# The first two gate/up pairs of the first 1024 tokens as four units of seven block products, run in phases

## The chip, the cores and the metric

One core of one Trainium2 chip runs the whole program. The metric is the device time of one execution in microseconds (us). A core has five engines with a queue each: PE multiplies matrices, DVE and ACT work on rows, POOL and SP mostly start transfers (DMAs). Each queue runs in its own order; semaphores make one wait for another.

## The reference

For 2048 tokens of width 1024 the reference mixes a local attention and a gated MLP, token by token:

```python
g = sigmoid((x * gate_w).sum(-1, keepdims=True))
qkv = x @ wqkv                                   # 32 heads of 32, window of 8 keys, every second token
a = attention(q, k, v) @ wo
b = (gelu(x @ w_gate) * (x @ w_up)) @ w_down     # inner width 3584
out = g * a + (1 - g) * b
```

All is in bf16, and `gelu` is the tanh form.

## The kernel before

**Tiles and stages.** The tokens are taken in two halves of 1024 (`SUP`), each half as two chunks of 512 columns (`SC`). The inner width of 3584 is cut into 14 pairs of 256 columns. First come the gate and up products of pair 0 and pair 1 for the first 1024 tokens, then queries and keys, values, and the rest of the pairs; then `down` (L1070) multiplies with `w_down` and `wo`. Large tiles lie in one tile called arena, at places given in KB (the R_ constants). PSUM, where PE writes, is one tile of eight banks, each 128 x 512 in f32.

**Seven block products.** A `Unit` (L360) multiplies a 256-column stripe of weights with 1024 tokens as a 2 x 2 block product with seven products instead of eight: L11, L12, L22 are blocks of the weights, S1 to S4 sums of blocks (`sums_pair`, L318), and R11, R12, R21, R22 are blocks of the transposed tokens, with T1 to T4 their differences (`x_forms`, L196, and `x_form3`). A product is four matmuls of 128x128 by 128x512. Its methods come in the order `p1` (L11), `p5` (S1), `p26` (L12 and S2), `p73` (S3 and S4) and `p4` (L22). Between them ACT copies a bank into another bank, where the next product is added to it (L384, L396), or into SBUF (L389, L374). In `p73` DVE adds one SBUF tile to two banks at once (L403): its operand is one access pattern that steps from bank Z to bank Y. `p4` adds into bank Y again, so it comes after this.

**The head.** `load_xn` brings rows of tokens, `pe_transpose_chunk` (L208) transposes 128x128 pieces on PE, four to a group, into one of four banks in turn, and DVE and ACT take turns to copy a group into SBUF (L219, L217). Pair 0 is computed plainly by `plain_pair` (L240), eight products for each 512 tokens: chunk 0 is transposed, multiplied, chunk 1 is transposed, and multiplied (L342 to L348). In between are `patterns` (small constant tiles), `x_forms`, `sums_pair` for pair 1, `gate_chunk` (the token gate's product) and `h_store` (gelu times up, L253). SP issues the loads in the order of the code: tokens of chunk 0, pair 0 in halves of 128 columns (256-byte rows), tokens of chunk 1, pair 1 in whole (512-byte rows), four blocks of the query/key weights (L336), and sixteen transposing loads of the other 1024 tokens (L340). Of these SP may have eight under way, since eight semaphores go round.

**The loop over units** (L1249) then runs all units with an overlap of one: `p1` of a unit, `p73` of the one before, `p5`, `p26`, `p4` of the one before. Pair 1 is its units 0 and 1 (`Q0` = 2), the queries and keys begin with unit 2. After each unit `run_bg` (L442) lets background tasks for DVE take steps, in order of priority, until a credit of 4.7 to 4.8 us is spent, by costs that the tasks state. `due` forces a task to its end ahead of a unit. Among the tasks are `sums_qk` (L456, sums of query/key weight blocks, priority 1), `h_task`, `late_forms`, `qk_prods` (products of queries and keys, L598) and `t_forms` (L864, differences of `w_down` blocks, L874), which has the lowest priority. `tf_close` (L886), at the end of unit `Q0` + 11, runs what is left of its first five steps at once.

Of the kernel before, what the change touches and what calls it, by code (L numbers as in the profile page):

```python
# [68 lines left out]
def kernel(  # L69
# [33 lines left out]
    def reg(kb, n):  # L103
        o = int(kb * KB)
        return arena[:, o:o + n]
# [12 lines left out]
    def bank(i):  # L118
        return banks[:, i, :]
# [17 lines left out]
    with tc.manual_schedule(engines={mybir.EngineType.PE, mybir.EngineType.DVE, mybir.EngineType.Activation,  # L137
# [11 lines left out]
        for i in range(NWARM):  # L149
            pw = bank(2 + i % 3)  # L150
            nc.tensor.matmul(pw, lhsT=warm[:, 0:P], rhs=warm, start=True, stop=True)
# [9 lines left out]
        sums1 = reg(R_W0 + 16, 4 * 2 * HK * P).rearrange("p (f m k n) -> p f m k n", f=4, m=2, k=HK)  # L161

        def load_pair(dst, i, split=False):
            c0 = 2 * P * i
            for (a, b) in (((0, P), (P, 2 * P)) if split else ((0, 2 * P),)):
                for m, src in ((0, B_w_gate), (1, B_w_up)):
                    nc.sync.dma_start(out=dst[:, m, :, a:b],
                                      in_=src[:, c0 + a:c0 + b].rearrange("(k p) n -> p k n", p=P))
# [3 lines left out]
        load_pair(raw0, 0, True)  # L172
        load_xn(1)
        load_pair(raw1, 1)
# [31 lines left out]
        ne = [0]  # L206

        def pe_transpose_chunk(c, dst):  # L208
            for j in range(4):
                for k0 in range(0, KT, 4):  # L210
                    p_ = bank((6, 7, 1, 5)[ne[0] % 4]).bitcast(BF16)[:, 0:SC].rearrange("p (a b) -> p a b", a=4)
                    for kk in range(4):
                        nc.tensor.transpose(out=p_[:, kk, :], in_=xn[c % 2][:, j, (k0 + kk) * P:(k0 + kk + 1) * P],
                                            identity=ident[:])
                    d = dst[:, k0:k0 + 4, j * P:(j + 1) * P]
                    if ne[0] % 2 == 1:
                        nc.scalar.copy(out=d, in_=p_)  # L217
                    else:
                        V.tensor_copy(out=d, in_=p_)  # L219
                    ne[0] += 1  # L220
# [12 lines left out]
        p5_n = [0]  # L233
# [5 lines left out]

        def plain_pair(w, G, U, s, half, xc):  # L240
            cs = slice(half * SC, (half + 1) * SC)
            for f in range(2):
                pg, pu = bank((0, 5)[f]), bank((3, 4)[f])
                for kt in range(KT):
                    nc.tensor.matmul(pg, lhsT=w[:, 0, kt, f * P:(f + 1) * P], rhs=xc[:, kt, :],
                                     start=(kt == 0), stop=(kt == KT - 1))
                nc.scalar.activation(out=G[:, f, cs], in_=pg, func=ACT.Gelu_apprx_tanh)
                for kt in range(KT):
                    nc.tensor.matmul(pu, lhsT=w[:, 1, kt, f * P:(f + 1) * P], rhs=xc[:, kt, :],
                                     start=(kt == 0), stop=(kt == KT - 1))  # L250
                nc.scalar.copy(out=U[:, f, cs], in_=pu)  # L251
# [16 lines left out]
        def patterns():  # L268
            with nc.allow_low_precision("block pattern of zeros and ones"):
                V.tensor_reduce(out=R_[:], in_=ident[:].rearrange("p (h d) -> p h d", d=4), axis=AX.X, op=ALU.add)  # L270
            pgw = bank(7).bitcast(BF16)[:, 0:KT]
# [63 lines left out]
        for i, (col, k0) in enumerate(((0, 0), (0, HK), (D, 0), (D, HK))):  # L335
            nc.sync.dma_start(out=wq[i], in_=A_wqkv[k0 * P:(k0 + HK) * P, col:col + D].rearrange("(k p) n -> p k n", p=P))  # L336
# [16 lines left out]

# [6 lines left out]
        class Unit:  # L360
# [15 lines left out]
            def p1(self):  # L376
                f = self.f
                self.T = self.dst()
                n = self.n
                self.X = bank((0, 5)[n % 2] if two[0] or n < Q0 else 0)  # L380
                self.yi = (2, 4)[n % 2]
                self.V, self.Y, self.Z = bank(1), bank(self.yi), bank(3)
                self.mm(self.X, "L11", f.R11, True)
                nc.scalar.copy(out=self.Y, in_=self.X)  # L384

            def p5(self):
                self.mm(self.V, "S1", self.f.T1, True)
                self.p5s = p5_tile()
                nc.scalar.copy(out=self.p5s, in_=self.V)  # L389

            def p26(self):
                f = self.f
                self.mm(self.X, "L12", f.R21, False)
                self.evac(self.T[:, 0, c1s], self.X)
                self.mm(self.Y, "S2", f.T2, False)
                nc.scalar.copy(out=self.Z, in_=self.Y)  # L396

            def p73(self):
                f = self.f
                self.mm(self.Y, "S3", f.T3, False)  # L400
                self.mm(self.Z, "S4", f.R22, False)
                pair = _win_ap(self.Z, [[(self.yi - 3) * SC, 2], [1, SC]])
                TT(out=self.T[:, :, c2s], in0=pair,  # L403
                   in1=self.p5s.rearrange("p (o n) -> p o n", o=1).to_broadcast([P, 2, SC]), op=ALU.add)
# [94 lines left out]
        def add_gu(w, sm, i, s):  # L499
            tg = tu = st_tile  # L500
            if i == 1 and s == 0:
                tg, tu = lambda: reg3(R_PROD, 2, SUP), lambda: reg3(R_PROD + 4, 2, SUP)
            ug = add_unit(gu_forms(w, sm, 0), xf[s], "gate", tg)
            uu = add_unit(gu_forms(w, sm, 1), xf[s], "up", tu)
            uu.fin = lambda: bg(h_task(ug.T, uu.T, i, s), *((5.5, now[0]) if (i, s) == (NPAIR - 1, 0) else (7.5 if i == NPAIR - 1 else 0, now[0] + 1)))
# [743 lines left out]
        for b in range(n):  # L1249
# [4 lines left out]
            prv = units[b - 1] if b > 0 else None  # L1254
            cur.p1()
            if prv:
                prv.p73()
# [11 lines left out]
            if prv:  # L1269
                prv.p4()  # L1270
# [37 lines left out]
```

## Time and profile before

| What | us |
|---|---|
| median of 3 runs (lowest, highest) | 720.98 (720.17, 722.09) |
| the profiled execution | 720.06 |
| its span, first to last instruction | 718.3 |
| PE busy in the span | 707.2 |
| DVE busy in the span | 673.2 |
| ACT busy in the span | 328.7 |
| first matmul of pair 0, of pair 1 (from the span's start) | 7.41, 25.06 |

A row of a timeline gives the start, the length, the engine, the line, what is done on which tiles, and how many instructions are merged; in brackets stands how long the engine sat idle before and what ended that. Matmuls are pipelined, so eight of 0.38 us each take less than eight times that; the distance from row to row is what they cost.

### The profile page before, as it was taken

Reading aid. Unit: us, or ns where it says so; the run is one execution under the profiler, and the core shown is the slowest. Engines: PE = TensorE matmul, PEld = TensorE weight load, DVE = VectorE, ACT = ScalarE, POOL = GpSimd, SP = SyncE. Lnnn points to the kernel's source line nnn. Section 1 sums busy time; section 2 is a strip of 40 time slices with the busy share of each in tenths; the row PEclk is TensorE's granted clock in tenths of the full one; section 3 lists DMA queues with packets and bytes.
Section 4 is the critical chain, followed back from the end, with each engine's and each line's share of the span. In section 5 each row is a group of like instructions: output and inputs, shape, how many; then the busy total and the mean of one; then the engine's idle time right before and its main releaser. Section 6 shows DMA issues by size and latency. Waiting matters only on the chain. (4 is left out here: it accounts for less than half of the span.)

```text
span 718.3 us, 10752 instructions
## 1 busy us (share of the span) xinstructions
PE 707.2 (98%) x4051; PEld 408.2 (57%) x4107; DVE 673.2 (94%) x722; ACT 328.7 (46%) x600; POOL 134.5 (19%) x233
## 2 busy tenths in 40 slices
PE   8999999999999999999999999999999999999998
PEld 4466656655544444444444444444447886758887
DVE  2789989999999999999999999999999999899997
ACT  4554546444456665555555555555322321131431
POOL 1323544133210332121300000000210002110011
PEclk9999999999999999999999999999999999999999
DMA  9976643378264758574934836371891899995951
GB/s 276 284 183 219 229 142 122 106 247 304 102 205 127 231 197 252 175 221 149 294 115 152 280 123 214 124 288 59 300 427 52 307 401 396 420 429 223 379 213 60
DMA packets 92276, 162.04 MB, mean 226 GB/s; under 512 B 19280, under 2 KB 68848, under 8 KB 87872
## 3 DMA queue, kind: packets, MB, share of 16 engines
q1 hardware_dynamic: 75520, 105.46, 42.7%
q0 software_dynamic: 15984, 48.29, 19.3%
q10 hardware_dynamic: 720, 7.60, 2.7%
q8 instruction: 32, 0.52, 0.3%
q14 instruction: 20, 0.16, 0.1%
HBM read 112.17 MB, written 54.14 MB: 232 GB/s over the span
## 5 line engine op out<-in xcount | busy, mean ns | idle before, releaser
L366 PE MATMUL banks<-arena 128*128 128x512 bf16 x2136 | 472.1, 379 | 4.2 <-DVE arena L403 0.7
L366 PEld LDWEIGHTS <-arena 128*128 128x128 bf16 x2184 | 240.5, 111 | 235.3 <-issue 7.0
L1046 PE MATMUL banks<-arena 128*128 128x256 bf16 x1260 | 138.9, 273 | 0.8 <-DVE arena L1012 0.6
L1046 PEld LDWEIGHTS <-arena 128*128 128x128 bf16 x1260 | 123.1, 98 | 16.7 <-issue 1.5
L389 ACT COPY arena<-banks 128x512 f32<-128x512 f32 x78 | 45.8, 587 | 130.7 <-PE banks L366 130.7
L403 DVE TENSOR_TENSOR arena<-banks,arena 128x1024 bf16<-128x1024 f32 x78 | 95.2, 1221 | 11.0 <-PE banks L366 5.5
L374 ACT CAST arena<-banks 128x512 bf16<-128x512 f32 x102 | 59.7, 586 | 42.4 <-PE banks L366 42.4
L745 DVE TENSOR_TENSOR arena<-arena 128x2048 bf16<-128x2048 bf16 x64 | 77.0, 1220 | 0.5
L752 DVE TENSOR_TENSOR arena<-arena 128x2048 bf16<-128x2048 bf16 (+2 forms) x96 | 73.9, 776 | 1.0
L598 DVE TENSOR_TENSOR arena<-arena 128x2048 bf16<-128x2048 bf16 x64 | 74.7, 1219 | 0.1
L260 POOL DMA_DIRECT2D h_d<-arena x28 | 20.4, 730 | 226.5 <-DVE arena L254 195.4
L1079 PE MATMUL banks<-arena 128*128 128x512 bf16 x282 | 62.5, 379 | 0.3
L396 ACT COPY banks<-banks 128x512 f32<-128x512 f32 x78 | 44.5, 570 | 21.8 <-PE banks L366 20.0
L1004 DVE TENSOR_TENSOR arena<-arena 128x2304 bf16<-128x2304 bf16 x40 | 53.3, 1352 | 0.5
L384 ACT COPY banks<-banks 128x512 f32<-128x512 f32 x78 | 45.0, 576 | 13.6 <-PE banks L366 12.1
L1051 ACT COPY banks<-banks 128x256 f32<-128x256 f32 x60 | 21.4, 356 | 60.9 <-PE banks L1046 60.7
L1079 PEld LDWEIGHTS <-arena 128*128 128x128 bf16 x288 | 28.2, 98 | 33.5
L927 DVE TENSOR_TENSOR arena<-arena 128x2048 bf16<-128x2048 bf16 (+1 forms) x40 | 41.8, 1111 | 1.3 <-DMA arena<-h_d 1.3
L372 ACT ACTIVATE arena<-banks 128x512 bf16<-128x512 f32 x54 | 32.2, 597 | 15.4 <-PE banks L366 15.3
L323 DVE TENSOR_TENSOR arena<-arena 128x1024 bf16<-128x1024 bf16 x60 | 38.6, 685 | 0.5
L1012 DVE TENSOR_TENSOR arena<-arena 128x2304 bf16<-128x2304 bf16 x28 | 37.7, 1351 | 0.2
L254 DVE TENSOR_TENSOR arena<-arena 128x2048 bf16<-128x2048 bf16 x28 | 34.0, 1216 | 1.9 <-ACT arena L251 1.4
(93 smaller groups left out, 435.8 us busy)
## 6 DMA issues: line engine op xcount, KB each, us to landing
arena<-t_d SPq DMA_DIRECT2D x8, 2304.0 KB, 14.4
h_d<-arena POOLq DMA_DIRECT2D x28, 512.0 KB, 4.3
arena<-w_c SPq DMA_DIRECT2D x12, 1152.0 KB, 14.1
t_d<-arena POOLq DMA_DIRECT2D x36, 256.0 KB, 4.3
arena<-h_d SPq DMA_DIRECT2D x6, 1536.0 KB, 12.7
arena<-in_B_w_gate_dram SPq DMA_DIRECT2D x15, 512.0 KB, 5.7
arena<-in_B_w_up_dram SPq DMA_DIRECT2D x15, 512.0 KB, 5.3
arena<-in_B_w_down_dram SPq DMA_DIRECT2D x28, 256.0 KB, 6.6
```

Of the source, the lines that this page charges most:

```text
L366: self.pe = nc.tensor.matmul(ps, lhsT=self.L[form](kt), rhs=rhs[:, kt, :], start=(start and kt == 0), stop=(kt == HK - 1), skip_group_chec ...
L374: nc.scalar.copy(out=o_, in_=i_)
L384: nc.scalar.copy(out=self.Y, in_=self.X)
L389: nc.scalar.copy(out=self.p5s, in_=self.V)
L396: nc.scalar.copy(out=self.Z, in_=self.Y)
L403: TT(out=self.T[:, :, c2s], in0=pair, in1=self.p5s.rearrange("p (o n) -> p o n", o=1).to_broadcast([P, 2, SC]), op=ALU.add)
L598: TT(out=dst, in0=q.rearrange("p (o s) -> p o s", o=1).to_broadcast([P, NWIN, AC]), in1=_win_ap(k, [[-DIL, NWIN], [1, AC]]), op=ALU.mult)
L745: TT(out=prod2[(t // 2) % 2][:, t % 2], in0=ab, in1=_win_ap(v[:, t, HALO:HALO + AC], [[SJ, NJ], [-DIL, NWIN], [1, SJ]]), op=ALU.mult)
L752: TT(out=out_, in0=h(0), in1=h(1), op=ALU.add)
L1004: TT(out=o_, in0=a, in1=b_, op=op)
L1046: nc.tensor.matmul(c(i, h, j), lhsT=l[:, kt, j * P:(j + 1) * P], rhs=r[:, kt, :], start=False, stop=(kt == KH - 1), skip_group_check=True)
L1079: nc.tensor.matmul(ps, lhsT=L[:, i, j * P:(j + 1) * P], rhs=R[:, i, :], start=(start and q == 0), stop=(q == NK - 1), skip_group_check=not ...
```

## The change

Pair 0 becomes two units as well, and the four units of pairs 0 and 1 run ahead of the loop in a new function, `head`, phase by phase: the same product for several units, then the next. The loop over units starts at `Q0`; the last of the four units still gets its `p73` and `p4` there. The units' banks are given by hand: X, V, Y, Z are (0, 3, 2, 0), (1, 5, 6, 1), (3, 0, 7, 3) and (5, 1, 4, 5). Outputs of pair 0 go to another place in the arena, and so do `p5`'s four results. Chunk 1 is transposed into two banks, each of them in two halves, and in another order. Pair 1 is loaded in halves too: the first halves of both pairs, the tokens of chunk 1, then the second halves. The query/key blocks are loaded with L21 and L22 ahead of L11 and L12. The four steps of the first part of `sums_qk` and two of the four of the second run in `head`. `h_store` of pair 0 becomes a background task from unit `Q0` + 1 on.

```diff
-            pw = bank(2 + i % 3)
+            pw = bank((2, 4, 6, 7)[i % 4])
...
-        sums1 = reg(R_W0 + 16, 4 * 2 * HK * P).rearrange("p (f m k n) -> p f m k n", f=4, m=2, k=HK)
-
-        def load_pair(dst, i, split=False):
+        sums0, sums1 = (reg(o, 4 * 2 * HK * P).rearrange("p (f m k n) -> p f m k n", f=4, m=2, k=HK)
+                        for o in (R_WQK + 48, R_W0 + 16))
+
+        def load_pair(dst, i, a=0, b=2 * P):
             c0 = 2 * P * i
-            for (a, b) in (((0, P), (P, 2 * P)) if split else ((0, 2 * P),)):
-                for m, src in ((0, B_w_gate), (1, B_w_up)):
-                    nc.sync.dma_start(out=dst[:, m, :, a:b],
-                                      in_=src[:, c0 + a:c0 + b].rearrange("(k p) n -> p k n", p=P))
+            for m, src in ((0, B_w_gate), (1, B_w_up)):
+                nc.sync.dma_start(out=dst[:, m, :, a:b], in_=src[:, c0 + a:c0 + b].rearrange("(k p) n -> p k n", p=P))
 
         gwr = small.tile([KT, P], BF16, tag="gwr", bufs=1)
         nc.gpsimd.dma_start(out=gwr[:], in_=gate_w.rearrange("(k p) -> k p", p=P))
-        load_pair(raw0, 0, True)
+        load_pair(raw0, 0, 0, P)
+        load_pair(raw1, 1, 0, P)
         load_xn(1)
-        load_pair(raw1, 1)
+        load_pair(raw0, 0, P, 2 * P)
+        load_pair(raw1, 1, P, 2 * P)
...
-        ne = [0]
-
-        def pe_transpose_chunk(c, dst):
-            for j in range(4):
-                for k0 in range(0, KT, 4):
-                    p_ = bank((6, 7, 1, 5)[ne[0] % 4]).bitcast(BF16)[:, 0:SC].rearrange("p (a b) -> p a b", a=4)
-                    for kk in range(4):
-                        nc.tensor.transpose(out=p_[:, kk, :], in_=xn[c % 2][:, j, (k0 + kk) * P:(k0 + kk + 1) * P],
-                                            identity=ident[:])
-                    d = dst[:, k0:k0 + 4, j * P:(j + 1) * P]
-                    if ne[0] % 2 == 1:
-                        nc.scalar.copy(out=d, in_=p_)
-                    else:
-                        V.tensor_copy(out=d, in_=p_)
-                    ne[0] += 1
+        def pe_transpose_chunk(c, dst, slots, by_k):
+            order = [(j, k0) for j in range(4) for k0 in range(0, KT, 4)]
+            if by_k:
+                order.sort(key=lambda g: g[1])
+            for n_, (j, k0) in enumerate(order):
+                i, o = slots[n_ % 4]
+                p_ = bank(i).bitcast(BF16)[:, o * SC:(o + 1) * SC].rearrange("p (a b) -> p a b", a=4)
+                for kk in range(4):
+                    nc.tensor.transpose(out=p_[:, kk, :], in_=xn[c % 2][:, j, (k0 + kk) * P:(k0 + kk + 1) * P],
+                                        identity=ident[:])
+                d = dst[:, k0:k0 + 4, j * P:(j + 1) * P]
+                if n_ % 2 == 1:
+                    nc.scalar.copy(out=d, in_=p_)
+                else:
+                    V.tensor_copy(out=d, in_=p_)
...
-        for i, (col, k0) in enumerate(((0, 0), (0, HK), (D, 0), (D, HK))):
+        for i, col, k0 in ((2, D, 0), (3, D, HK), (0, 0, 0), (1, 0, HK)):
...
-        G0, U0 = st_tile(), st_tile()
-        pe_transpose_chunk(0, xf[0].c1)
-        plain_pair(raw0, G0, U0, 0, 0, xf[0].c1)
-        patterns()
-        pe_transpose_chunk(1, xf[0].c2)
-        list(x_forms(0))
-        list(sums_pair(raw1, sums1))
-        plain_pair(raw0, G0, U0, 0, 1, xf[0].c2)
-        for c in range(2):
-            gate_chunk(c, bank(6 + c))
-        h_store(G0, U0, 0, 0)
-        x_form3(0)
...
+                self.lie((0, 5)[n % 2] if two[0] else 0, 1, (2, 4)[n % 2], 3)
+                self.p1_()
+
+            def lie(self, x, v, y, z):
+                self.X, self.V, self.Y, self.Z = (bank(i) for i in (x, v, y, z))
+                self.yz = y - z
+
+            def p1_(self):
+                self.mm(self.X, "L11", self.f.R11, True)
                 nc.scalar.copy(out=self.Y, in_=self.X)
 
-            def p5(self):
+            def p5(self, t=None):
                 self.mm(self.V, "S1", self.f.T1, True)
-                self.p5s = p5_tile()
+                self.p5s = p5_tile() if t is None else t
                 nc.scalar.copy(out=self.p5s, in_=self.V)
 
+            def p2(self):
+                self.mm(self.X, "L12", self.f.R21, False)
+                self.evac(self.T[:, 0, c1s], self.X)
+
+            def p6(self):
+                self.mm(self.Y, "S2", self.f.T2, False)
+                nc.scalar.copy(out=self.Z, in_=self.Y)
...
-                pair = _win_ap(self.Z, [[(self.yi - 3) * SC, 2], [1, SC]])
+                pair = _win_ap(self.Z, [[self.yz * SC, 2], [1, SC]])
...
-        sqk = bg(sums_qk(0), 1, 1)
-        due(Q0, sqk)
-        at_end(0, lambda: (sqk.step(), sqk.step()))
-        due(Q0 + 1, bg(sums_qk(1), 1, 2))
+        sq0, sq1 = sums_qk(0), sums_qk(1)
+        due(Q0 + 1, bg(sq1, 1, Q0))
...
-        for b in range(n):
+        def head():
+            xs, f = xf[0], []
+            for w, sm, o in ((raw0, sums0, R_ATTN), (raw1, sums1, R_PROD)):
+                for m in range(2):
+                    u = Unit(gu_forms(w, sm, m), xs, ("gate", "up")[m], None)
+                    u.T = reg3(o + 4 * m, 2, SUP)
+                    f.append(u)
+            units[0:Q0] = f[2:]
+            for u, x, v, y, z in zip(f, (0, 1, 3, 5), (3, 5, 0, 1), (2, 6, 7, 4), (0, 1, 3, 5)):
+                u.lie(x, v, y, z)
+            f[3].fin = lambda: bg(h_task(f[2].T, f[3].T, 1, 0), 0, now[0] + 1)
+            T = lambda o_, a, b_: TT(out=flat(o_), in0=flat(a), in1=flat(b_), op=ALU.subtract)
+            s0, s1 = sums_pair(raw0, sums0), sums_pair(raw1, sums1)
+
+            pe_transpose_chunk(0, xs.c1, ((0, 0), (1, 0), (3, 0), (5, 0)), False)
+            f[0].p1_()
+            f[1].p1_()
+            patterns()
+            f[0].p2()
+            f[1].p2()
+            f[2].p1_()
+            f[3].p1_()
+            pe_transpose_chunk(1, xs.c2, ((0, 0), (1, 0), (0, 1), (1, 1)), True)
+            T(xs.T1, xs.R12, xs.R11)
+            next(s0)
+            next(s1)
+            f[2].p2()
+            f[3].p2()
+            for c in range(2):
+                gate_chunk(c, bank(c))
+            next(s0)
+            T(xs.T2, xs.R22, xs.T1)
+            next(s1)
+            T(xs.T3, xs.R22, xs.R12)
+            for i, u in enumerate(f):
+                u.p5(regf(R_XN + 2 * i, SC))
+            for g in (s0, s0, s1, s1):
+                next(g)
+            T(xs.T4, xs.R21, xs.T2)
+            for u in f:
+                u.p6()
+            next(sq0)
+            next(sq0)
+            for u in f[:3]:
+                u.p73()
+            for g in (sq0, sq0, sq1, sq1):
+                next(g)
+            for u in f[:3]:
+                u.p4()
+            bg(h_task(f[0].T, f[1].T, 0, 0), 0, Q0 + 1)
+
+        head()
+        for b in range(Q0, n):
             now[0] = b
             for fn in hooks.pop(b, []):
                 fn()
             cur = units[b]
-            prv = units[b - 1] if b > 0 else None
+            prv = units[b - 1]
```

More of the change, by code (lines that the diff above doesn't have):

```diff
@@ L231, in st_first @@
             return st_tile()
-        p5_n = [0]
+        p5_n = [2]
         def p5_tile():
@@ L238, in p5_tile @@
             return regf((R_P5A[p5_n[0] > NX0 + 1], R_P5B)[k], SC)
[L240 to L251, printed above, removed]
         def h_store(G, U, i, s):
@@ L270, in patterns @@
                 V.tensor_reduce(out=R_[:], in_=ident[:].rearrange("p (h d) -> p h d", d=4), axis=AX.X, op=ALU.add)
-            pgw = bank(7).bitcast(BF16)[:, 0:KT]
+            pgw = bank(5).bitcast(BF16)[:, 0:KT]
             nc.tensor.transpose(out=pgw, in_=gwr[:], identity=ident[0:KT, 0:KT])
@@ L376, in p1 @@
             def p1(self):
-                f = self.f
                 self.T = self.dst()
                 n = self.n
[L380 to L383, printed above, removed]
+                self.lie((0, 5)[n % 2] if two[0] else 0, 1, (2, 4)[n % 2], 3)
[5 more added lines that the diff above has]
+                self.mm(self.X, "L11", self.f.R11, True)
                 nc.scalar.copy(out=self.Y, in_=self.X)
-            def p5(self):
+            def p5(self, t=None):
                 self.mm(self.V, "S1", self.f.T1, True)
-                self.p5s = p5_tile()
+                self.p5s = p5_tile() if t is None else t
                 nc.scalar.copy(out=self.p5s, in_=self.V)
-            def p26(self):
[L392 to L396, printed above, removed]
+            def p2(self):
[4 more added lines that the diff above has]
+                nc.scalar.copy(out=self.Z, in_=self.Y)
+            def p26(self):
+                self.p2()
+                self.p6()
             def p73(self):
@@ L499, in add_gu @@
         def add_gu(w, sm, i, s):
[L500 to L504, printed above, removed]
+            ug = add_unit(gu_forms(w, sm, 0), xf[s], "gate", st_tile)
+            uu = add_unit(gu_forms(w, sm, 1), xf[s], "up", st_tile)
             uu.fin = lambda: bg(h_task(ug.T, uu.T, i, s), *((5.5, now[0]) if (i, s) == (NPAIR - 1, 0) else (7.5 if i == NPAIR - 1 else 0, now[0] + 1)))
@@ L1253 @@
             cur = units[b]
-            prv = units[b - 1] if b > 0 else None
+            prv = units[b - 1]
             cur.p1()
-            if prv:
-                prv.p73()
+            prv.p73()
             cur.p5()
@@ L1268 @@
                 actq.pop(0)()
-            if prv:
-                prv.p4()
+            prv.p4()
             for fn in post.pop(b, []):
```

## The prediction

> **What bounds the kernel now.** I read the page's first part, then the timelines of PE, DVE and ACT over the first 45 us (start, length, engine and line, operation, tiles, count, idle time before), then DVE around 112 us.
>
> ```profile
> PE 707.2 (98%) x4051; PEld 408.2 (57%) x4107; DVE 673.2 (94%) x722; ACT 328.7 (46%) x600; POOL 134.5 (19%) x233
> ```
>
> PE is busy 98% of 718.3 us: a product taken away is time taken away, and so is a wait put in. DVE, at 94%, is close behind. PE in the head:
>
> ```profile
> 4.41 1.38 PE L213 MATMUL banks<-ident,arena 128*128 128x128 bf16 x16 [0.47 <-DMA arena<-in_A_x_dram]
> 6.05 1.07 PE L213 MATMUL banks<-ident,arena 128*128 128x128 bf16 x16 [0.26 <-DVE arena L219]
> 7.41 1.89 PE L245 MATMUL banks<-arena 128*128 128x512 bf16 x8 [0.29 <-DVE arena L219]
> ...
> 14.51 2.32 PE L213 MATMUL banks<-ident,arena 128*128 128x128 bf16 x32
> 17.09 1.89 PE L245 MATMUL banks<-arena 128*128 128x512 bf16 x7 [0.25 <-DVE arena L219]
> ...
> 25.06 17.88 PE L366 MATMUL banks<-arena 128*128 128x512 bf16 x80
> 43.37 1.95 PE L366 MATMUL banks<-arena 128*128 128x512 bf16 x8 [0.43 <-DVE arena L463]
> ```
>
> See three things. Eight matmuls take 1.72 us from row to row (7.41 to 9.13), 0.2157 each. The second chunk of tokens holds PE from 14.51 to 17.09, 2.57 us. At 43.37 PE waits for DVE: the 80 before it end at 42.94, so their last starts 0.38 earlier and the next was due at 42.78; lost 0.59. DVE and ACT beside it:
>
> ```profile
> 15.10 1.32 DVE L219 COPY arena<-banks 128x512 bf16<-128x512 bf16 x3
> ...
> 17.07 3.81 DVE L199 TENSOR_TENSOR arena<-arena 128x2048 bf16<-128x2048 bf16 x3
> 20.80 2.61 DVE L323 TENSOR_TENSOR arena<-arena 128x1024 bf16<-128x1024 bf16 x4
> ...
> 29.08 2.36 DVE L463 TENSOR_TENSOR arena<-arena 128x2048 bf16<-128x2048 bf16 x2 [1.92 <-DMA arena<-in_A_wqkv_dram]
> 31.39 1.23 DVE L403 TENSOR_TENSOR arena<-banks,arena 128x1024 bf16<-128x1024 f32 x1
> ```
> ```profile
> 15.33 2.13 ACT L217 COPY arena<-banks 128x512 bf16<-128x512 bf16 x4 [0.23 <-PE banks L213]
> ```
>
> A DVE copy out of PSUM takes 0.42 to 0.43 us, ACT's 0.59; a 128x2048 form 1.14 back to back (two in 2.36 with the last 1.22 long), a 128x1024 sum 0.605, the two-bank sum of `p73` ("TT" below) 1.22.
>
> **The change, part by part**, against the profiled execution (span 718.3, 720.06 us).
>
> *Products.* Pair 0 was 64 matmuls, 8 x 4 x 2; two units are 2 x 7 x 4 = 56. Eight gone at 0.2157: **-1.73 us**. All are on PE's path. The warm-up, the transposes and the gate products keep their number.
>
> *First loads.* Up to the second chunk the bytes come in the old places, with pair 1's first half where pair 0's second was. The first up half of pair 0 lands at 8.85 (issued 2.17, 6.7 to landing); before, it was first used at 9.13; now the second unit's first product is due after four matmuls, 7.41 + 0.86 = 8.27, and waits to 8.90: **+0.63**. The four halves before the change land at 7.1, 8.85, 9.5 and 10.65, 1.18 apart; four more behind the second chunk's tokens (last at 13.4) end at 18.1, where pair 1 in whole rows ended at 17.0. DVE reaches pair 1's first sum at 18.6 (below): no wait, by 0.5. The price with that cover gone: if a half took 1.77, as a whole load did (13.4 to 17.0), it lands at 20.5, and everything behind it on DVE is 1.9 late. A gain is excluded, since DVE would wait for nothing there anyway. The query/key weights come about 1.1 later, L21 and L22 at 20.8 and 24.8 by the old spacing; DVE asks at 26.3. On SP's queue the sixteen transposing DMAs and all behind move by the same 1.1; their reader comes two tasks later too.
>
> *Second chunk of transposes.* PE comes to it at 8.90 + 0.86, the gate transpose 0.1, four products 3.45: 13.32. Its eight groups of four now have two banks, in two halves each, instead of four banks. In the changed program's order of instructions each group waits for the copy of the group two before it, which is the one in the other half of its bank, not the one four before it. A step in ACT's bank is 0.42 from a group's first transpose to its copy (14.91 to 15.33), 0.59 the copy, 0.05 to the next transpose (the copy ending 15.91, PE at 15.96): 1.06. The four groups there need three steps, and 0.22 at each end: 3.6, 3.67 with ACT's own queue ahead. PE goes on at 16.99. **+1.10** against 2.57. From below: nothing, if the halves handed over as four banks do.
> [...] No run here yet shows two halves in use.
>
> *The four two-bank sums (TT).* DVE, after the last copy at 16.86: T1 1.14, three sums 1.82, T2 1.14, one sum 0.605, T3 1.14, four sums 2.42, T4 1.14, two query/key sums 2.28: the first TT runs from 28.54 to 29.77. PE, from 16.99: two products 1.73, gates 0.98 (24.08 to 25.06), eight products 6.90, three 2.59: at 29.19 it is at the second unit's S4 product, into bank 1. In the changed program this product waits for the first TT, though that TT needs banks 0 and 2: its operand spans from one to the other, and bank 1 lies between. Likewise the third unit's S4 product (bank 3) waits for the second TT (banks 1 and 6), and the second unit's last product (bank 6) for the third TT (3 and 7). The first wait is 29.82 - 29.19 = 0.63. In the second and third, the TT can only begin 0.20 after the product just before, takes 1.22, and 0.05 to PE, against 0.86 of PE's own work: 0.61 each. **+1.85**. Behind the waiting product are all of PE's; DVE itself then waits for PE. From below: 0.61 x 2, with DVE early; from above 1.85 + 1.9 by the load above.
>
> *Handover to the loop.* Half of the L21 differences are done in the head, so S4 of the first query unit no longer waits: **-0.59**. DVE has two TTs (2.45) and four sums (2.42) more to do, which fill its idle 1.40, 1.92 and 2.55 us before 37.44. ACT and POOL get work beside PE; ACT is busy 46%, POOL 19%.
>
> *Around 112 us.* The planner gave t_forms less room earlier, since the new h task stands where it ran:
>
> ```profile
> 105.86 0.70 DVE L683 TENSOR_TENSOR banks<-banks,arena 128x512 f32<-128x512 f32 x1 [0.40 <-PE banks L603]
> ...
> 112.65 1.22 DVE L403 TENSOR_TENSOR arena<-banks,arena 128x1024 bf16<-128x1024 f32 x1
> 113.79 0.68 DVE L874 TENSOR_TENSOR arena<-arena 128x1024 bf16<-128x1024 bf16 x1
> 114.39 0.29 DVE L305 TENSOR_SCALAR go<-zs 128x8 bf16<-128x8 f32 x2
> 114.53 4.63 DVE L598 TENSOR_TENSOR arena<-arena 128x2048 bf16<-128x2048 bf16 x4
> 119.07 1.22 DVE L403 TENSOR_TENSOR arena<-banks,arena 128x1024 bf16<-128x1024 f32 x1
> ```
>
> Where one t_forms operation (L874) stands before, the changed order has three: `tf_close` forces what is left. DVE was tied to PE at 105.86 and has no idle time after it, so an earlier lead doesn't help. The TT ends at 120.29; the copy of the product that waits for it starts at 121.57, so that product (0.65 to its last matmul, 0.38, 0.04) starts at 120.51: 0.17 to spare after 0.05. Two more operations of 0.60 to 0.72: 1.2 to 1.44, less 0.17: **+1.15**. From below nothing (DVE ahead by 1.4), from above 1.3.
>
> *Sum:* -1.73 + 0.63 + 1.10 + 1.85 - 0.59 + 1.15 = **+2.4 us**. On the profiled execution: 722.5; on the median of the three runs, 0.92 above it: **723.4 us**. Below 0.3%, 2.16 us, a measurement of this kernel can't tell a change from none.
>
> **Rivals.**
> - *The stall near 119 us is covered*: DVE reaches 112 us ahead. For it: idle 0.81 before 89.98 and 1.30 before 92.50. Against: the wait for PE at 105.86. 722.2.
> - *The guards cost nothing*, the end on the other side: bank halves and spanned banks hold nobody up. Place: the second chunk and the S4 products. Price: 1.10 and 1.85 gone, +2.4 becomes -0.5, 720.4. It decides at DVE's first TT: if DVE is done with it before 29.19 and the next two before PE asks. Against: the waits are in the program's order, and 0.61 needs no lateness of DVE.
> - *Loads late*: +1.9, 725.3. For: halves have twice the packets. Against: the 1.18 spacing.
> - *The array's clock falls back*: the six warm-up matmuls took 2.74 us, about 0.42 apart, twice 0.2157, and PE reached full pace at 5.1. If 3.7 us of half-filled transposes undid this, the next 3.9 us (1.2 to 5.1) would run at half pace, +1.9: 725.3. Against: 3.0 us of transposes with gaps (4.41 to 7.41) are followed by matmuls at 0.2157. [...]
> - *The saving isn't there*: excluded, the changed order has eight matmuls fewer.
>
> **Chances.** Forecast 0.56 (its own range 722.4 to 724.6, bound inside, six in ten of it slower), covered stall 0.17, free guards 0.08, loads 0.10, clock 0.07, something unseen that gains 0.02. Slower by over 0.3%: 0.34 + 0.02 + 0.17 = 0.53; faster 0.02; within 0.45. The range reaches from between the free guards and the covered stall, 721.2, to the late loads, 725.4.
>
> **What would show it.** PE's 32 transposes taking 3.6 us, not 2.6, with idle time put down to the DVE and ACT copies; a 0.6 us wait for the up load near 8.3; three waits for TT near 29, 32 and 34; no wait for the query/key sums near 43; a 1.1 us wait for TT near 121. Wrong would be: PE going from transposes to products at twice 0.2157, DVE waiting for pair 1's load at 18 us, or more PE idle time after 125 us than before.

## The result, and the profile after

| | before | after |
|---|---|---|
| median of 19 runs each, us (lowest, highest) | 720.26 (719.89, 722.09) | 722.09 (721.82, 722.95) |
| profiled execution, us | 720.06 | 721.98 |
| its span, us | 718.3 | 720.2 |
| PE's first product, us | 7.41 | 7.20 |
| the two-bank sum that before has at 44.12, us | 44.12 | 45.32 |
| the product that before has at 120.51 (worked out in the forecast), us | 120.51 | 122.98 |
| the product that before has at 663.32, us | 663.32 | 665.75 |

The changed kernel takes 1.0022 times as long (95% interval 1.0015 to 1.0029): 1.83 us more, which lies within 0.3%. The forecast was +2.4. Read row by row, the table says where it came from: +1.20 up to the sum at 44 us, +1.27 more up to 121 us, nothing from there to 665 us (+2.47 and +2.43), and then -0.5 back in the last 55 us, where the two programs have the same instructions.

The page's first part, the head of PE's timeline (start, length, engine and line, operation, tiles, count, idle time before), and DVE's two-bank sums:

```profile
PE 709.1 (98%) x4099; PEld 407.1 (57%) x4099; DVE 677.8 (94%) x728; ACT 330.9 (46%) x603; POOL 134.0 (19%) x233
```
```profile
7.20 1.04 PE L341 MATMUL banks<-arena 128*128 128x512 bf16 x4 [0.29 <-DVE arena L221]
8.76 1.04 PE L341 MATMUL banks<-arena 128*128 128x512 bf16 x4 [0.52 <-DMA arena<-in_B_w_up_dram]
...
13.30 0.61 PE L215 MATMUL banks<-ident,arena 128*128 128x128 bf16 x8
14.27 0.73 PE L215 MATMUL banks<-ident,arena 128*128 128x128 bf16 x8 [0.37 <-DVE arena L221]
15.17 1.28 PE L215 MATMUL banks<-ident,arena 128*128 128x128 bf16 x12 [0.17 <-DVE arena L221]
16.74 0.38 PE L215 MATMUL banks<-ident,arena 128*128 128x128 bf16 x4 [0.28 <-ACT arena L219]
16.96 1.89 PE L341 MATMUL banks<-arena 128*128 128x512 bf16 x8
...
29.95 1.89 PE L341 MATMUL banks<-arena 128*128 128x512 bf16 x8 [0.52 <-DVE arena L387]
32.36 1.89 PE L341 MATMUL banks<-arena 128*128 128x512 bf16 x8 [0.52 <-DVE arena L387]
34.69 13.54 PE L341 MATMUL banks<-arena 128*128 128x512 bf16 x62 [0.45 <-DVE arena L387]
```
```profile
28.67 1.23 DVE L387 TENSOR_TENSOR arena<-banks,arena 128x1024 bf16<-128x1024 f32 x1
31.08 1.23 DVE L387 TENSOR_TENSOR arena<-banks,arena 128x1024 bf16<-128x1024 f32 x1 [1.18 <-PE banks L341]
33.42 1.23 DVE L387 TENSOR_TENSOR arena<-banks,arena 128x1024 bf16<-128x1024 f32 x1 [1.11 <-PE banks L341]
```

PE's weight loads (PEld, one for each matmul) are 4107 before and 4099 now: eight matmuls fewer. (PE's own count before, 4051, is no measure: 56 matmul records are missing there.) Idle times in brackets understate a loss, since the last matmul before still shows 0.38 us; a loss is read from row to row. The second unit's first product was due at 7.20 + 4 x 0.2157 = 8.06 and came at 8.76: 0.70. The second chunk holds PE from 13.30 to 16.96, 3.66, with idle time put down to the copies of DVE and ACT; it was 2.57. Eight matmuls from 29.95 end at 31.68, and the next come at 32.36: 0.68. By the same reckoning the first wait is 0.69 (due 29.26) and the third, at 34.69, is 0.60: 1.97 together. In DVE's rows the second and the third sum wait for PE, and PE for the sum before: they take turns.

The wait for the query/key sums at 43 us is gone. PE, and DVE around 112 us:

```profile
39.66 12.68 PE L341 MATMUL banks<-arena 128*128 128x512 bf16 x58
```
```profile
113.84 1.22 DVE L387 TENSOR_TENSOR arena<-banks,arena 128x1024 bf16<-128x1024 f32 x1
114.98 2.13 DVE L853 TENSOR_TENSOR arena<-arena 128x1024 bf16<-128x1024 bf16 x3
117.03 0.24 DVE L293 TENSOR_SCALAR go<-zs 128x8 bf16<-128x8 f32 x2
117.17 4.62 DVE L579 TENSOR_TENSOR arena<-arena 128x2048 bf16<-128x2048 bf16 x4
121.72 1.21 DVE L387 TENSOR_TENSOR arena<-banks,arena 128x1024 bf16<-128x1024 f32 x1
```
```profile
122.98 1.24 PE L341 MATMUL banks<-arena 128*128 128x512 bf16 x5 [1.11 <-DVE arena L387]
```

Where one form stood before (L874), three stand now (L853, x3), and PE stands idle 1.11 us for the sum behind them; from row to row the product at 122.98 is 1.27 late.

### The profile page after: what moved, and what is told of

The parts are those of the page before. It is cut to its first block, busy times and chain, and to the rows that moved or that the text cites. A ratio compares the mean times of both kernels' runs of the same rounds, so it can differ in the third digit from the quotient of the medians.

```text
span 720.2 us, 10802 instructions
## 1 busy us (share of the span) xinstructions
PE 709.1 (98%) x4099; PEld 407.1 (57%) x4099; DVE 677.8 (94%) x728; ACT 330.9 (46%) x603; POOL 134.0 (19%) x233
## 5 line engine op out<-in xcount | busy, mean ns | idle before, releaser
L341 PE MATMUL banks<-arena 128*128 128x512 bf16 x2240 | 488.0, 379 | 4.5 <-DVE arena L387 3.3
L341 PEld LDWEIGHTS <-arena 128*128 128x128 bf16 x2240 | 245.8, 110 | 244.9 <-issue 10.7
L1025 PEld LDWEIGHTS <-arena 128*128 128x128 bf16 x1260 | 123.1, 98 | 16.3 <-issue 1.1
L387 DVE TENSOR_TENSOR arena<-banks,arena 128x1024 bf16<-128x1024 f32 x80 | 97.6, 1220 | 11.8 <-PE banks L341 7.8
L1058 PE MATMUL banks<-arena 128*128 128x512 bf16 x288 | 62.8, 379 | 0.0
L376 ACT COPY banks<-banks 128x512 f32<-128x512 f32 x80 | 45.6, 570 | 23.5 <-PE banks L341 20.3
L363 ACT COPY banks<-banks 128x512 f32<-128x512 f32 x80 | 46.1, 576 | 14.9 <-PE banks L341 13.9
L1058 PEld LDWEIGHTS <-arena 128*128 128x128 bf16 x288 | 28.2, 98 | 33.6
L311 DVE TENSOR_TENSOR arena<-arena 128x1024 bf16<-128x1024 bf16 x64 | 41.1, 685 | 0.5
```

What stands on the lines that cost most here:

```text
L341: self.pe = nc.tensor.matmul(ps, lhsT=self.L[form](kt), rhs=rhs[:, kt, :], start=(start and kt == 0), stop=(kt == HK - 1), skip_group_chec ...
L387: TT(out=self.T[:, :, c2s], in0=pair, in1=self.p5s.rearrange("p (o n) -> p o n", o=1).to_broadcast([P, 2, SC]), op=ALU.add)
L1025: nc.tensor.matmul(c(i, h, j), lhsT=l[:, kt, j * P:(j + 1) * P], rhs=r[:, kt, :], start=False, stop=(kt == KH - 1), skip_group_check=True)
L1058: nc.tensor.matmul(ps, lhsT=L[:, i, j * P:(j + 1) * P], rhs=R[:, i, :], start=(start and q == 0), stop=(q == NK - 1), skip_group_check=not ...
```

## The experiments

Times below are against the kernel before as it ran beside each experiment (medians 720.13 to 720.28); the changed kernel itself stands at +1.83.

**The three waits: is it the spanned bank?** The banks are handed out so that no unit's bank lies between another's two (the banks of the warm-up, the transposes and the gate products move with them; "..." stands for code left out):

```diff
...
-            for u, x, v, y, z in zip(f, (0, 1, 3, 5), (3, 5, 0, 1), (2, 6, 7, 4), (0, 1, 3, 5)):
+            for u, x, v, y, z in zip(f, (0, 2, 4, 6), (4, 6, 0, 2), (1, 3, 5, 7), (0, 2, 4, 6)):
...
-            pe_transpose_chunk(1, xs.c2, ((0, 0), (1, 0), (0, 1), (1, 1)), True)
+            pe_transpose_chunk(1, xs.c2, ((0, 0), (2, 0), (0, 1), (2, 1)), True)
...
```

> The changed kernel with each head unit's two result banks next to each other (0 and 1, 2 and 3, 4 and 5, 6 and 7), so that the two-bank sum of one unit no longer has a bank of another unit between its two. Nothing else moves. My theory (the three waits near 29, 32 and 34 us are guards on a bank that merely lies between the two that the sum reads): all three waits, 0.69 + 0.68 + 0.60, are gone, and no wait takes their place: about -1.9 us against the changed kernel, some 720.2, level with the kernel before. Rival (DVE is simply late or slow with these sums, and PE has to wait for their results): the order and the lengths on DVE are unchanged, so the waits stay, 722.1. A mixed outcome, in which the first wait of 0.69 stays and the other two go, would give 720.8.

Measured: 720.4 against 720.13, ratio 1.0003 (0.9993 to 1.0013): 1.6 us of the 1.83 are gone. PE and DVE of this kernel:

```profile
20.43 29.74 PE L341 MATMUL banks<-arena 128*128 128x512 bf16 x137
```
```profile
29.34 1.22 DVE L387 TENSOR_TENSOR arena<-banks,arena 128x1024 bf16<-128x1024 f32 x1
31.07 1.23 DVE L387 TENSOR_TENSOR arena<-banks,arena 128x1024 bf16<-128x1024 f32 x1 [0.50 <-PE banks L341]
...
49.33 1.23 DVE L200 TENSOR_TENSOR arena<-arena 128x2048 bf16<-128x2048 bf16 x1 [0.68 <-DMA arena<-in_A_x_dram]
```

137 matmuls in one row: none of the three waits is left. The second unit's S4 is matmul 45 of that row and starts at 20.43 + 44 x 0.2157 = 29.92, while DVE's first sum runs until 30.56. DVE was as late as ever and nobody waited: it was the spanned bank. (In this profile the first gate load let PE start 0.35 later, and PE waited 1.02 us for the up load and not 0.70. Of the 1.97 that leaves 1.30, and the profiled span is 1.3 shorter. The last row shows a form that waits 0.68 us for tokens; it returns below.)

**The second chunk: what are halves of a bank worth?** Two runs. In one all groups use the first half of each bank; in the other the chunk goes ahead of the third and fourth unit's first products, when four banks are free (DVE's sums behind it are put in another order to fit).

```diff
-            pe_transpose_chunk(1, xs.c2, ((0, 0), (1, 0), (0, 1), (1, 1)), True)
+            pe_transpose_chunk(1, xs.c2, ((0, 0), (1, 0), (0, 0), (1, 0)), True)
```

> The changed kernel with the second chunk's eight transpose groups all in the first half of the two banks, so that there are two buffers and not four. Theory (a half that is free can't be written while the other half of its bank is being copied, so the second halves bring nothing): the chunk takes 3.66 us as with the halves, and the time is that of the changed kernel. Rival (the halves do hand over one by one and something else made the chunk slow): with half the buffers the chunk grows by about the 1.1 us that two banks more are worth, to some 4.7.

```diff
-        load_pair(raw1, 1, 0, P)
         load_xn(1)
+        load_pair(raw1, 1, 0, P)
...
+            pe_transpose_chunk(1, xs.c2, ((3, 0), (5, 0), (0, 0), (1, 0)), False)
+            T(xs.T1, xs.R12, xs.R11)
+            T(xs.T2, xs.R22, xs.T1)
             f[2].p1_()
             f[3].p1_()
-            pe_transpose_chunk(1, xs.c2, ((0, 0), (1, 0), (0, 1), (1, 1)), True)
-            T(xs.T1, xs.R12, xs.R11)
...
```

> The changed kernel with the second chunk of tokens transposed ahead of the third and fourth unit's first products, when four banks are free, in the order of the kernel before (one group to a bank, no halves); the chunk's tokens are loaded ahead of pair 1's first half; DVE's forms T1 and T2 follow the transposes at once. The banks of the sums stay as in the changed kernel. Theory for the transposes (two banks in two halves are two buffers, not four): the chunk takes 2.2 to 2.6 us, not 3.66, a gain of 1.1 to 1.4. Rival (halves hand over as banks do, and the chunk was slow for the DVE and ACT copies' sake): it stays at 3.6. The same run parts two theories of the three waits near 30 us: DVE comes to the first sum over 2 us earlier here, but the spanned bank is still there. By the spanned bank all three waits stay, 0.6 each (in sum 1.8 against 1.97 before); by DVE's lateness the first goes altogether and the sum falls to 1.2 or less. By both of my theories the time is 722.1 - 1.2 = about 720.8 (720.5 to 721.0); by the rivals 722.1 or, with the first wait gone alone, 721.4.

Measured: with one half 722.7 (one time), with four banks 720.85 against 720.13, ratio 1.0009 (1.0000 to 1.0018). The chunk in the kernel with one half:

```profile
13.87 0.61 PE L215 MATMUL banks<-ident,arena 128*128 128x128 bf16 x8
14.85 0.73 PE L215 MATMUL banks<-ident,arena 128*128 128x128 bf16 x8 [0.37 <-DVE arena L221]
15.75 1.28 PE L215 MATMUL banks<-ident,arena 128*128 128x128 bf16 x12 [0.17 <-DVE arena L221]
17.31 0.38 PE L215 MATMUL banks<-ident,arena 128*128 128x128 bf16 x4 [0.28 <-ACT arena L219]
17.53 1.89 PE L341 MATMUL banks<-arena 128*128 128x512 bf16 x8
```

From 13.87 to 17.53 it is 3.66 again, idle time for idle time: half the buffers, and nothing changes in the chunk. (That this one run took 0.6 us more than the changed kernel goes back to the first loads: the chunk starts 0.57 later, at 13.87 and not 13.30.) With four banks:

```profile
11.57 2.28 PE L215 MATMUL banks<-ident,arena 128*128 128x128 bf16 x32
13.69 3.62 PE L341 MATMUL banks<-arena 128*128 128x512 bf16 x16
...
18.21 1.90 PE L341 MATMUL banks<-arena 128*128 128x512 bf16 x8
20.37 7.94 PE L341 MATMUL banks<-arena 128*128 128x512 bf16 x36 [0.26 <-DVE arena L311]
28.84 1.89 PE L341 MATMUL banks<-arena 128*128 128x512 bf16 x8 [0.52 <-DVE arena L387]
```

2.12 us without a wait. Of the 1.54 saved, 0.43 come back at 20.37 (due at 18.21 + 1.73), where PE now waits for a weight sum; the gain is 1.1. The halves' rival falls twice. The other question of this run was not answered: DVE did not come early, since it waited 0.28 and 0.55 us for loads, and its first sum came at 27.56, right behind its other work. The three waits stayed (0.70, 0.68, 0.61), which fits both theories of them, the spanned bank and a late DVE; the run with the banks side by side decides between them.

**The forced forms.** Pair 0's multiplication is planned one unit earlier, into DVE's idle time:

```diff
-            bg(h_task(f[0].T, f[1].T, 0, 0), 0, Q0 + 1)
+            bg(h_task(f[0].T, f[1].T, 0, 0), 2, Q0)
```

> The changed kernel with the multiplication of pair 0's two results planned one unit earlier, where DVE stands idle for 2.62 us before the sum at 45.3 us. In DVE's order the forms that are forced ahead of the sum near 119 us are then one instead of three. Theory (the two more forced forms make that sum late, and PE waits for it): two forms of 0.71 less ahead of the sum, so the wait of 1.11 us before PE's product at 122.98 is gone: -1.1 us, about 721.0. Rival (DVE's work up to that sum is the same in amount, so it is late there in any case): the wait stays, 722.1. Second rival: the multiplication makes the sum at 45.3 late, which costs PE 0 to 0.5 there and keeps the gain below 0.6.

Measured: 720.93 against 720.13, ratio 1.0008 (0.9999 to 1.0017): -1.0. DVE and PE of this kernel:

```profile
113.78 1.22 DVE L387 TENSOR_TENSOR arena<-banks,arena 128x1024 bf16<-128x1024 f32 x1
114.92 0.68 DVE L853 TENSOR_TENSOR arena<-arena 128x1024 bf16<-128x1024 bf16 x1
...
120.20 1.22 DVE L387 TENSOR_TENSOR arena<-banks,arena 128x1024 bf16<-128x1024 f32 x1
```
```profile
119.91 6.20 PE L341 MATMUL banks<-arena 128*128 128x512 bf16 x28 [0.31 <-ACT banks L363]
```

One form is forced, the sum comes 1.52 earlier, and PE runs through. The product at 178.20 comes at 176.86, 0.06 of it from an earlier start: 1.28 gained, the whole of what the step had cost. A multiplication near 42 us was paid for at 121 us, because the planner's credit, not DVE's idle time, decides how many forms are done in between.

**The wait for the up load.** The first chunk's gate product goes into it:

```diff
...
+            patterns()
             f[0].p1_()
+            gate_chunk(0, bank(4))
             f[1].p1_()
-            patterns()
...
-            for c in range(2):
-                gate_chunk(c, bank(c))
+            gate_chunk(1, bank(1))
```

> The changed kernel with the small transpose of the gate weights ahead of the first unit's first product, and the first chunk's gate product (eight narrow matmuls, 0.49 us) between the first and the second unit's first products, that is, in the 0.70 us in which PE waits for pair 0's up weights. Theory (this wait is for a load that nothing moves, so work put into it is free): the second unit's first product still starts at 8.76 and everything behind it comes 0.49 + 0.10 earlier until the second chunk of transposes, whose tokens have landed by then: -0.5 to -0.6 us. But DVE's chain up to the first two-bank sum must come forward by the same amount for the gain to last; it hangs on the second chunk's last copy, which comes forward by 0.1 to 0.6 as well. So 721.5 to 721.7. Rival (the gain is given back at the first of the three sums, because DVE sets it): 722.1.

Measured: 721.78 against 720.13, ratio 1.0022 (1.0013 to 1.0031). PE of this kernel:

```profile
8.20 0.61 PE L270 MATMUL banks<-arena 128*32 128x512 bf16 x8
8.74 4.49 PE L341 MATMUL banks<-arena 128*128 128x512 bf16 x20
```

The second unit's first product starts at 8.74 with the gate product (L270) ahead of it, where it started at 8.76 without, so the work put there was free. The first wait for a two-bank sum grew to 0.86, and what is left at PE's row behind the third (34.25 against 34.69) is 0.44 in the profile; between the medians it is 0.2, within both intervals, so its size is open.

**The 0.5 us at the end.** In the profile of before the last output sums stand so (here of its second profile):

```profile
710.86 1.28 DVE L1216 TENSOR_TENSOR arena<-arena 128x512 f32<-128x512 f32 x2
712.58 0.69 DVE L1203 TENSOR_TENSOR omgrep<-banks,arena 128x512 bf16<-128x512 f32 x1 [0.44 <-issue]
713.19 0.68 DVE L1203 TENSOR_TENSOR arena<-banks,arena 128x512 bf16<-128x512 f32 x1
```

"issue" means that DVE waited for nothing that the profile shows. Six memsets are added to the kernel before, far away, at 1.2 us:

```diff
-        V.memset(zh, 0.0)
+        for _ in range(7):
+            V.memset(zh, 0.0)
```

> The kernel before with six more memsets of 128x64 zeros on DVE at 1.2 us, where DVE stands idle until 4.9; nothing else. It tests where the 0.54 us come from that the changed kernel and its variants save in the last 55 us, from the product at 663.3 to the end, in which the two programs have the same instructions: in the profile of before DVE sits 0.44 us ahead of one output sum at 712.2 with nothing shown that it waits for. Theory (it hangs on where the instruction stands in DVE's stream, as instructions are fetched in pieces; the changed stream is six longer): with six more the 0.44 goes, and the stretch is 54.4 us as after the change. Rival (it belongs to before for another reason, such as another engine's stream): 0.44 stays, 55.0. Second rival (it was a matter of that one execution): the kernel before, looked at again, shows 54.4 as well.

> The kernel before, unchanged, for a second profile beside the run with six more memsets. If the 0.44 us of idle time ahead of the output sum at 712.2 belongs to the program, it is there again, and the stretch from the product at 663.3 to the end is 55.0 us; if it was a matter of one execution, it may be gone, 54.4.

Measured: with six more 719.98, before again 720.41 (one time each). From the product at 663 us to the span's end: before 54.93, again 54.94, with six more 54.60, after the change 54.45. (By the unrounded spans the 0.54 of the first text above is 0.48.) With six more:

```profile
710.80 1.28 DVE L1217 TENSOR_TENSOR arena<-arena 128x512 f32<-128x512 f32 x2
712.17 0.69 DVE L1204 TENSOR_TENSOR omgrep<-banks,arena 128x512 bf16<-128x512 f32 x1
713.12 0.69 DVE L1204 TENSOR_TENSOR arena<-banks,arena 128x512 bf16<-128x512 f32 x1 [0.26 <-PE banks L1047]
```

The 0.44 belongs to the program before, not to one execution, and with six instructions more on DVE's queue it is gone, and 0.34 us of PE's time with it. So 0.34 of the 0.48 hang on where an instruction stands in DVE's stream, as far as one profile with six more can show it. The page of before has 32 and 20 packets of kind "instruction" over the span (queues q8 and q14, 0.52 and 0.16 MB), so instructions come in pieces; that these pieces make the 0.44 was not shown. The other 0.14 lie behind PE's last matmul (3.15 us to the span's end before, 3.02 after the change) and stay open.

**All together.** The four edits in one kernel, with chunk 2 in banks 4, 6, 0 and 2.

> The changed kernel with the four edits together: each unit's two result banks side by side, the second chunk of transposes in four banks with its tokens loaded earlier, the first gate product in the wait for the up weights, and pair 0's multiplication one unit earlier. If the waits are separate terms of one sum, the gains add up: 1.97 (three waits), 1.3 (the chunk at 2.3 instead of 3.66), 0.5 (gate product in the wait), 1.1 (forced forms), in all 4.9 us below the changed kernel, or 717.1 (716.7 to 717.7), 3 us below the kernel before. Rival: DVE, 94% busy over the span, becomes the bound in the head once PE's waits are gone, and part is given back in new waits for DVE between 18 and 46 us: 718 to 719.5.

Measured: 722.28 against 720.18, ratio 1.0028 (1.0015 to 1.0040): a miss of 5 us, and not the rival either. PE runs without a wait from 7.85 to 50.5, and then (DVE; PE; then windows of PE, with start and end in us, busy times by engine, PE's granted clock, DMA share and GB/s):

```profile
50.16 2.49 DVE L200 TENSOR_TENSOR arena<-arena 128x2048 bf16<-128x2048 bf16 x2 [4.66 <-DMA arena<-in_A_x_dram]
52.56 1.22 DVE L387 TENSOR_TENSOR arena<-banks,arena 128x1024 bf16<-128x1024 f32 x1
```
```profile
53.83 6.38 PE L341 MATMUL banks<-arena 128*128 128x512 bf16 x21 [3.30 <-DVE arena L387]
```
```profile
53.80:54.80 1.00, 0.97 (x5) 0.68 (x5) 1.00 (x2) 0.57 (x1) 0.73 (x2) 0.99 1.04 350
54.80:55.80 1.00, 1.00 (x4) 0.37 (x3) 1.00 (x2) 0.90 (x4) 0.37 (x1) 0.50 1.07 371
...
57.00:58.00 1.00, 1.00 (x3) 0.33 (x2) 0.94 (x10) 0.17 (x1) 0.00 (x0) 0.50 1.10 350
58.00:60.00 2.00, 2.00 (x10) 1.32 (x9) 1.14 (x2) 0.00 (x0) 0.00 (x0) 0.95 0.49 166
```

Two things. DVE comes to the form T2 of the second 1024 tokens at 45.5, with PE and DVE over 3 us ahead of the changed kernel (its sum at 45.32 comes at 42.00 here). But the last of the sixteen transposing loads that bring these tokens, which SP starts about 1.3 us apart (in the changed kernel most follow one another at 1.30, of which 1.26 is the issue itself), lands at 50.03. It landed at 46.84 before and at 48.09 in the changed kernel, so it did not come forward with the rest; it came 1.9 later, and why is open. PE waits 3.30 us for the sum behind T2. The sign was there in the run with the banks side by side, where this form waited 0.68 us for the same loads. And then the array's clock falls: five matmuls at 0.215, then matmuls 0.427 apart, granted clock 0.50 from 54.8 to 58.2, about 1.7 us lost. Not every execution loses it: five of the six runs have a mean granted clock of 0.997 or 0.998, and the sixth, with 1.000, took 720.74, which is 1.5 below the median. The next kernel puts three query-key multiplications ahead of T2, and the one after puts T1 ahead of these (its loads had landed by 44 us: here it starts at 44.27 and waits for none). Each diff is against the run before it:

```diff
-                due(n_ + 4, bg(qk_prods(units[n_], s, t), 2, n_ + 2))
+                due(n_ + 4, bg(qk_prods(units[n_], s, t), 2, n_ + (1 if n_ == Q0 else 2)))
```

> The four edits together, as in the run before, with one more: the first three query-key multiplications are planned one unit earlier, so that DVE has them to do at 44 to 48 us, ahead of the form T2, which there waited 4.66 us for the last transposing loads of x (landed at 50.03, whatever PE does). Theory: that run lost 3.30 us in PE's wait for the sum behind T2, and another 1.6 us because after this idle time the array ran eight matmuls at half pace (0.427 us each instead of 0.216); both hang on T2's place alone. With T2 behind the sum, both go: 722.3 - 4.9 = 717.4 (717.0 to 718.2), 2.8 us below the kernel before. Rival (the loads bound this stretch in any order, since DVE's work from T2 to the sum near 120 us is fixed in amount and starts at 50.0): the wait comes back at a later sum, with 1 to 3 us, 718.5 to 720.5.

```diff
-                due(n_ + 4, bg(qk_prods(units[n_], s, t), 2, n_ + (1 if n_ == Q0 else 2)))
+                due(n_ + 4, bg(qk_prods(units[n_], s, t), *((3.5, n_ + 1) if n_ == Q0 else (2, n_ + 2))))
...
-            for g in x_forms(1):
+            for i, g in enumerate(x_forms(1)):
                 yield 1.24
+                if i == 0:
+                    yield None
```

> The five edits of the run before, with DVE's form T1, whose loads are in by 44 us, ahead of the three query-key multiplications instead of behind them. There DVE stood idle for 1.64 us (45.58) until ACT had copied out the unit that the multiplications read, and PE later waited 1.29 us (51.40) for the sum behind T1. Theory (T1 fits into this idle time): the sum comes 1.13 earlier, and so does PE: 718.7 - 1.1 = 717.6. Rival (the loads of x or the sum's own product set this place): no change, 718.7.

Measured: 718.73 against 720.15, ratio 0.9978 (0.9969 to 0.9987), and 717.77 against 720.28, ratio 0.9966 (0.9954 to 0.9978). In the first of the two the clock stays at 1.0 and the wait behind T2 is gone: T2 runs from 51.37, behind the sum, with no idle time before it; but 1.29 us are left at the same sum, since the multiplications had to wait for ACT. So 717.4 was missed, and this is the rival's time for another reason than the rival's. The second comes within 0.2 us of the 717.6 expected. DVE of the first, and PE of both:

```profile
45.58 3.50 DVE L579 TENSOR_TENSOR arena<-arena 128x2048 bf16<-128x2048 bf16 x3 [1.64 <-ACT arena L349]
```
```profile
51.40 0.81 PE L341 MATMUL banks<-arena 128*128 128x512 bf16 x3 [1.29 <-DVE arena L387]
```
```profile
50.87 9.44 PE L341 MATMUL banks<-arena 128*128 128x512 bf16 x43 [0.16 <-DVE arena L387]
```

The last version is 2.5 us faster than the kernel before and 4.3 faster than the changed one. By the sum, 1.73 of the 2.5 are the eight products: they do show, once the waits are out of the way.

## Why the prediction was right, and where a size was off

It said +2.4 us, and gave 0.53 to slower by over 0.3% and 0.45 to within 0.3%. It came to +1.83, within 0.3%, by the mechanisms that it named. The measured 722.09 lies inside the whole range (721.2 to 725.4) and just below the forecast's own (722.4 to 724.6). By the time alone the rival of the covered stall (722.2) fits better; only the rows show that the stall came and that something else was gained.

- *Products, -1.73*: eight weight loads fewer, at the same pace (the 62 matmuls from 34.69 fill 13.54 us, 0.2157 from one to the next).
- *Up load, +0.63*: 0.70 here; between 0.41 and 1.02 in the four variants that leave it in place, as the first loads land at other times in each.
- *Chunk, +1.10*: 1.09 (3.66 against 2.57). Both bounds were tried: one half gives the same (3.66), four banks take it all away (2.12). The program's waits go by bank and not by half: that is what the 3.66 with and without second halves shows, and the 1.09 is what they cost against the four banks of before. No run leaves these waits out, so none shows whether the chip needs them.
- *Three sums, +1.85*: 1.97, since the third was 0.60 and the others 0.69 and 0.68. The cause is shown: banks side by side, no wait. The wait is one of the program's own, put on all banks between the operand's ends.
- *Handover, -0.59*: no wait at 43 us.
- These give +1.44 with the measured sizes; PE's first product came 0.21 earlier in the profile of after, so 1.23, and 1.20 is what the sum at 44 us shows. The forecast had 1.26.
- *Forms, +1.15*: 1.27, and 1.28 when undone. The rival of the covered stall falls with it, although its time is the nearest.
- *Loads late* did not come: pair 1's last halves landed at 17.58 and 18.29 (forecast 18.1), and DVE waited for none.
- *The clock* did not fall after 3.66 us of half-filled transposes (PE busy for 2.71 of them): the eight matmuls from 16.96 on fill a row of 1.89, which is 7 x 0.2157 and 0.38, and the granted clock is 1.00 both in the chunk (13.30 to 16.96) and in these eight (16.96 to 18.68). The mean granted clock is 0.999 or 1.000 in all nineteen runs. The fall itself exists: it came in an experiment after 3.30 us of real idleness, and shows there as 0.997 or 0.998 in five runs of six.

The step that was off is one that the sum did not have: it took everything behind 125 us as unchanged, since the instructions are. It gained 0.48, of which 0.34 hang on six more instructions on DVE's queue. So 2.4 became 1.9 between the profiled executions and 1.83 between the medians. The other part of the miss in absolute time (723.4 against 722.09) is the base: the three runs shown had a median of 720.98, 0.92 above the profiled execution, and nineteen have 720.26, 0.20 above it.

## What to carry to other kernels

Before a two-bank operand is formed, look at the banks between its ends: the program's waits held them too (0.69, 0.68 and 0.60 us here, no wait with the banks side by side), so a unit's banks belong side by side. Two buffers in one bank were worth one here (3.66 us for the chunk with either), since the program's waits go by bank. When a stage is shortened by several microseconds, look for the first thing that does not move with it (here transposing loads that SP starts 1.3 us apart): a wait of 3.3 us cost 5 where the array's clock fell behind it, in five runs of six.

## What the runs showed of the hardware that was not expected

- After 3.30 us without a matmul the array went on at 0.215 us a matmul for 0.9 us, and only then ran at half clock for 3.4 us (granted 1.00 in the idle time, 0.99 from 53.8 to 54.8, 0.50 from 54.8 to 58.2). By the mean granted clocks (0.997 or 0.998, once 1.000) the fall came in five of six runs. The wait of 1.29 us in the next kernel was followed by no such fall: its eleven runs have 1.000, once 0.999.
- An instruction near the end can wait 0.44 us for nothing shown, in both profiles of one program, and not at all when six small instructions are added 710 us earlier. Between these two builds 0.34 us of the time to the end went with it.
